# Gate and up of a SwiGLU layer by Strassen's 2 by 2 scheme, over pairs of token chunks

## The chip, the cores and the metric

One core of a Trainium2 chip runs the whole program. The metric is the device time of one execution in microseconds (us). Before the change it was 2166.83 us, the median of 3 runs that lay between 2162.72 and 2170.63.

The names of the engines are those of the profile: PE (TensorE, matmuls), PEld (its weight loads), DVE (VectorE), ACT (ScalarE), POOL (GpSimd), SP (SyncE, which here only issues DMAs). All five work through their own list of instructions in order.

## The reference

A transformer block on 2048 tokens of width 640: attention with 32 heads, then a SwiGLU layer of width 1728, each behind a layer norm and with a residual.

```python
B, S, D, H, F = 1, 2048, 640, 32, 1728
def _A_ref(x, wqkv, wo):                      # attention, Dh = 20
    q, k, v = qkv[0], qkv[1], qkv[2]
    p = _softmax(jnp.einsum("bhqd,bhkd->bhqk", q, k) * (Dh ** -0.5), axis=-1)
    o = jnp.einsum("bhqk,bhkd->bhqd", p, v)
    return o.transpose(0, 2, 1, 3).reshape(B, S, D) @ wo
def _B_ref(x, w_gate, w_up, w_down):
    g = _silu(x @ w_gate)
    u = x @ w_up
    return (g * u) @ w_down
h = x + _A_ref(_layernorm(x), A_wqkv, A_wo)
h2 = h + _B_ref(_layernorm(h), B_w_gate, B_w_up, B_w_down)
```

All is float32. The change is in `x @ w_gate` and `x @ w_up`.

## The kernel before

**Precision.** PE multiplies in the type fp32r. To keep float32's accuracy each operand is held as two fp32r parts, `hi` (a copy, rounded) and `lo` (what is left), and each product is made of three: hi by hi, lo by hi, hi by lo. `split` (L71) makes the parts: ACT writes `hi`, and POOL (or DVE, where the caller says so) subtracts and writes `lo`.

**Tiles.** The tokens are 4 chunks of 512 (`NC`, `CH`), each of 4 tiles of 128 (`TPC`). The width 640 is 5 blocks of 128 (`ND`), the inner width 1728 is 13 blocks of 128 and a last one of 64 (`NF` = 14, index f). A PSUM bank holds 128 x 512.

**Order.** The program is written in the order in which each engine is to work (`manual_schedule`), and nothing reorders it. Attention comes first and ends about 1550 us into the span. The output projection of chunks 0 and 1, their layer norm and their transposition (`projection`, L554: `project`, `apply`, `flip`) are woven into attention's last units. Chunk 2 (`two`, also called `ahead`) and chunk 3 (`three`) follow when attention is over, with the first gate products (`gate(0, c)`) between their steps to keep PE at work. The normalised, transposed tokens of a chunk, split into hi and lo, are `z2_c[c]`, five blocks of 128 x 512 for each part.

**The layer itself** (L861 to the end) runs over f, and for each f over the four chunks. `gate` (L832) makes the gate's 128 x 512 result in one bank with 15 matmuls (3 part products by 5 blocks) and the up result in another with 15 more; ACT takes Silu of the first (L849), DVE multiplies (`product`, L854), ACT and POOL split the product into `y_hi` and `y_lo` (`parts`). `down` (L917) multiplies a y of three chunks earlier by the rows of `w_down` for its f: for each of 4 token tiles two halves of 320 columns, each 3 matmuls into a bank that DVE adds to the residual `h_c[c]` (L932). For the last f, of 64, gate and up share one bank, and y has its two parts in the two halves of one tile.

**Weights.** `load_gate_up` loads 128 columns of gate and of up through one raw buffer, and ACT and POOL split them into `gu_hi` and `gu_lo`, one f ahead. They serve all four chunks, so each weight is loaded and split once. `load_down_raw` and `split_down` do the same for `w_down`. All loads go through SP's queue. There are 4 banks for gate and up (`ps_a`) and 4 for projections, transposes and down (`ps_b`).

## Time and profile before

| what | before |
|---|---|
| median of 3 runs | 2166.83 us |
| the profiled execution | 2168.25 us, of which its span is 2166.2 us |
| granted TensorE clock | 0.996 |
| share of the chain that ended last: PE | 92% |
| of it gate and up (L841) | 17% |
| of it down (L927) | 9% |
| GpSimd busy over the whole span | 15% |

The span runs from the first instruction to the last; the 2.05 us beside it lie outside the program's instructions. The profile is one execution, 1.4 us above the median of the runs.

How to read what follows. A row of a view by groups gives the source line, the engine, the operation, the tile written and the tiles read, the shapes, the count, then the busy time of the group in us and the mean of one in ns, then the idle time of that engine ahead of them and what ended it. A row of the timeline gives the start and the length in us. A matmul's end is modelled and overlaps the next one, so that what a stream of matmuls costs is read from the distance of their starts. In a window's row the busy time of each engine in that stretch stands with the number of instructions.

### The profile page before, as it was taken

To read this page: it belongs to the slowest core of one execution; us is meant where nothing else is said; L and a number is where in the kernel's file an instruction comes from. 1 tells how busy PE (TensorE), PEld (TensorE's weight loads), DVE (VectorE), ACT (ScalarE), POOL (GpSimd) and SP (SyncE) were. 2 spreads that over 40 slices of the span, in tenths; PEclk is the share of its full clock that TensorE was granted. 3 is DMA by queue.
4 is the path that set the end of the run, shared out by engine and by line. 5 is a ranking of instruction groups with operands and counts; after the bars stand their busy time and mean duration, and the time that the engine had idled before them with its cause. 6 is when DMAs were issued, how large, how long until landed. Compare 5 with 4: busy or idle time off the path is not lost.

```text
span 2166.2 us, 33813 instructions
## 1 busy us (share of the span) xinstructions
PE 2132.8 (98%) x12882; PEld 1254.5 (58%) x12882; DVE 1616.1 (75%) x2731; ACT 1277.6 (59%) x2486; POOL 317.0 (15%) x282
## 2 busy tenths in 40 slices
PE   7999999999999999999999999999999999999999
PEld 5766774333333333333333333355688888888888
DVE  6999996999999999999999999974354333544434
ACT  4222217999989999999999999977522111211110
POOL 5122212000000000000000001011223222122220
PEclk9999999999999999999999999999999999999999
DMA  7565532210302111102112122011221000010002
GB/s 250 160 178 165 164 106 80 58 48 19 87 19 61 44 36 55 48 22 79 26 47 59 49 67 53 22 58 58 77 62 37 25 25 25 19 31 25 25 19 97
DMA packets 123066, 140.06 MB, mean 65 GB/s; under 512 B 38600, under 2 KB 71624, under 8 KB 122904
## 3 DMA queue, kind: packets, MB, share of 16 engines
q1 hardware_dynamic: 109224, 111.68, 17.8%
q10 hardware_dynamic: 13680, 26.23, 4.0%
q8 instruction: 101, 1.65, 0.3%
q14 instruction: 61, 0.50, 0.1%
HBM read 99.06 MB, written 38.01 MB: 63 GB/s over the span
## 4 chain that ended last, share of the span: by engine, by line
PE 92%; DVE 5%; DMA 2%; ACT 0%; issue 0%; POOL 0%; SPq 0%; ACTq 0%; POOLq 0%; DVEq 0%
PE acc L656 23%; PE ps_a L841 17%; PE ps_max L156 15%; PE ps_one L646 13%; PE ps_b L927 9%; PE ps_one L397 5%; DVE mx L150 3%; PE ps_wide L146 2%; PE ps_one L431 2%; PE ps_max L586 2%; PE ps_b L586 1%; DVE mx L162 1%; PE ps_one L365 0%; PE ps_one L181 0%; DMA o_t<-o_d 0%
## 5 line engine op out<-in xcount | busy, mean ns | idle before, releaser
L652 ACT ACTIVATE probs<-ps_one 128x512 f32<-128x512 f32 x2048 | 1044.9, 623 | 133.6 <-PE ps_one L646 132.7
L162 DVE TENSOR_REDUCE mx<-ps_max 128x1 f32<-128x512 f32 x1632 | 1021.0, 683 | 97.9 <-PE ps_max L156 49.9
L646 PE MATMUL ps_one<-q_stk,k_stk 62*128 62x512 f32 x2048 | 551.7, 422 | 1.1 <-ACT e L240 0.7
L656 PE MATMUL acc<-probs,v_stk 128*32 128x512 f32 x4096 | 546.3, 605 | 0.2
L156 PE MATMUL ps_max<-k_stk,q_stk 60*128 60x512 f32 x1632 | 541.6, 460 | 2.5 <-DVE mx L162 1.5
L156 PEld LDWEIGHTS ps_max<-k_stk,q_stk 60*128 60x128 f32 x1632 | 230.6, 184 | 429.9 <-DVE mx L162 412.7
L932 DVE TENSOR_TENSOR h<-ps_b,h 128x320 f32<-128x320 f32 x448 | 194.6, 486 | 311.6 <-PE ps_b L927 311.5
L646 PEld LDWEIGHTS ps_one<-q_stk,k_stk 62*128 62x128 f32 x2048 | 299.7, 185 | 81.0 <-ACT probs L652 52.3
L841 PE MATMUL ps_a<-z,gu_hi 128*128 128x512 f32 x1080 | 276.0, 393 | 0.6 <-ACT z L72 0.6
L150 DVE TENSOR_REDUCE mx<-ps_wide 128x2 f32<-128x1024 f32 x208 | 240.6, 1217 | 17.8 <-PE ps_wide L146 17.4
L841 PEld LDWEIGHTS ps_a<-z,gu_hi 128*128 128x128 f32 x1080 | 200.4, 188 | 42.2 <-ACT z L72 0.8
L72 ACT ACTIVATE y_hi<-s 128x512 fp32r<-128x512 f32 (+1 forms) x56 | 35.4, 631 | 253.3 <-DVE s L854 246.8
L656 PEld LDWEIGHTS acc<-probs,v_stk 128*32 128x32 f32 x4096 | 80.9, 108 | 161.0 <-issue 152.6
L849 ACT ACTIVATE s<-ps_a 128x512 f32<-128x512 f32 (+1 forms) x56 | 33.4, 597 | 198.0 <-PE ps_a L841 198.0
L841 PE MATMUL ps_a<-z,gu_lo 128*128 128x512 f32 x540 | 142.2, 393 | 0.0
L927 PE MATMUL ps_b<-d_hi,y_hi 128*128 128x320 f32 x448 | 139.0, 311 | 0.0
L927 PE MATMUL ps_b<-d_lo,y_hi 128*128 128x320 f32 x448 | 138.1, 309 | 0.0
L927 PE MATMUL ps_b<-d_hi,y_lo 128*128 128x320 f32 x416 | 128.3, 308 | 0.0
L173 POOL CAST both<-neg 128x16 fp32r<-128x16 f32 x32 | 6.6, 206 | 806.3 <-DVE neg L169 388.1
L841 PEld LDWEIGHTS ps_a<-z,gu_lo 128*128 128x128 f32 x540 | 101.4, 188 | 23.2
L73 POOL TENSOR_TENSOR y_lo<-s,y_hi 128x512 fp32r<-128x512 f32 x52 | 67.8, 1304 | 268.9 <-ACT y_hi L72 268.9
L240 ACT ACTIVATE e<-ps_one 128x512 f32<-128x512 f32 x37 | 22.1, 596 | 119.5 <-PE ps_one L397 95.8
(118 smaller groups left out, 1623.2 us busy)
## 6 DMA issues: line engine op xcount, KB each, us to landing
raw<-qk_d SPq DMA_DIRECT2D x70, 160.0 KB
k_stk<-qk_d SPq DMA_DIRECT2D x64, 160.0 KB
q_stk<-qk_d SPq DMA_DIRECT2D x64, 160.0 KB
rb<-r_d SPq DMA_DIRECT2D x32, 256.0 KB
qk_d<-e ACTq DMA_DIRECT2D x22, 320.0 KB
v_d<-ev ACTq DMA_DIRECT2D x16, 384.0 KB
raw<-qk_d SPq DMA_DIRECT2D x70, 80.0 KB
v_stk<-v_d SPq DMA_DIRECT2D x28, 192.0 KB
```

Of the source, the lines that this page charges most:

```text
L73: lo_engine.tensor_tensor(out=lo, in0=src, in1=hi.bitcast(F32), op=ALU.subtract)
L150: nc.vector.tensor_reduce(mx[:, :, pair, t, kc], ps, axis=AX.X, op=ALU.max)
L156: nc.tensor.matmul(ps, queries[u][rows, pair, t * P : (t + 1) * P], keys[u // NC][rows, pair, kc * CH : (kc + 1) * CH], start=True, stop=True,
L162: nc.vector.tensor_reduce(mxs[u][:, b, pair, t, kc : kc + 1], ps, axis=AX.X, op=ALU.max)
L397: nc.tensor.matmul(ps, w[:, k, m * P : (m + 1) * P], a[:, k, :], start=(n == 0 and k == 0), stop=(n == 2 and k == ND - 1),)
L586: nc.tensor.matmul(ps[:, :HALF], a[:, k, :], w[:, k, hs], start=(n == 0), stop=(n == 3 * ND - 1),)
L646: nc.tensor.matmul(ps, keys[u // NC][rows, p, kt * P : (kt + 1) * P], queries[u][rows, p, :], start=True, stop=True,)
L652: nc.scalar.activation(probs[p][:, b, :], ps, AF.Exp, scale=scale)
L656: nc.tensor.matmul(acc[32 * j : 32 * j + 32, :], values[u // NC][:, kt, j * VW : j * VW + 32], probs[j // 2][:, j % 2, :], start=(kt == 0) ...
L841: nc.tensor.matmul(ps, a[:, i, k, :], b[:, k, :], start=(n == 0), stop=(n == 3 * ND - 1))
L927: nc.tensor.matmul(ps[:, :HALF], a[:, t * P : (t + 1) * P], b[:, hs], start=(n == 0), stop=(n == len(products) - 1),)
L932: nc.vector.tensor_tensor(out=h, in0=ps[:, :HALF], in1=h, op=ALU.add)
```

## The change

The gate and up products of a pair of chunks are seen as one product of 2 by 2 blocks. The weights' blocks are A11 and A12 (gate, token blocks 0 and 1, then 2 and 3) and A21 and A22 (up, the same); the tokens' blocks are B11 and B21 (the first chunk of the pair, token blocks 0 and 1, then 2 and 3) and B12 and B22 (the second chunk). In Winograd's form of the scheme seven products replace eight: of A11, A12, A22 and four sums of weights S1 to S4, with B11, B21, B22 and four sums of tokens T1 to T4. Each product is over two blocks of 128, so it takes 3 x 2 = 6 matmuls of 512 columns. The fifth block of 128 of the width is left out of the scheme and is added in the plain way by 3 matmuls for each of gate and up and each chunk ("K4").

An *element* is one f for one pair of chunks. The elements run over the pair 0 (chunks 0 and 1) with the narrow f first (done plainly, `plain`), then f = 0 to 12 (`blocks`), then the same for pair 1 (chunks 2 and 3). That gives:

- **Weights** are loaded and split twice, once for each pair (`Weights`). For each element but the narrow ones POOL makes S1 to S4 (four sums of 128 x 256, `sums`), and seven units of 128 x 256 and one of the fifth block are split by ACT and POOL, during the element ahead.
- **Results** come from seven banks: the eight sums of `blocks` are made on DVE out of PSUM (one is a copy on ACT), and the product of Silu and up (`mul`) now reads two tiles of SBUF.
- **Tokens of pair 0**: `quarter_sums` adds hi and lo back together on DVE, POOL makes the differences, ACT and DVE split them again. That stands between the projections of chunk 2.
- **Tokens of pair 1**: their layer norm, transposes, differences and splits (`late_tokens`) are moved from before the layer into elements 1 to 5, a step after every second product; the results go to DRAM (`z_d`, `t_d`). In the last element of pair 0 `swap` loads them over the tiles of pair 0, as each is read for the last time.
- **Down** of an element runs in the steps of the next, two halves of a tile behind each product (three in a narrow element). The banks are 5 for `ps_a` and 3 for `ps_b`.

The diff, cut to its core:

```diff
+    t14 = pe2.tile([P, 2, 4, CH], F32R, name="t14")
+    t32 = pe2.tile([P, 2, 4, CH], F32R, name="t32")
+        def sums(self):
...
+            tt = nc.gpsimd.tensor_tensor
+            tt(out=s1, in0=u[:, 0:2], in1=u[:, 2:4], op=ALU.add)
+            tt(out=s2, in0=s1, in1=g[:, 0:2], op=ALU.subtract)
+            tt(out=s3, in0=g[:, 0:2], in1=u[:, 0:2], op=ALU.subtract)
+            tt(out=s4, in0=g[:, 2:4], in1=s2, op=ALU.subtract)
+        def unit(self, kind):
...
+            t = self.units[kind] = pd1.tile([P, 2, 2, P], F32R, name="unit", bufs=9)
+            split(src, t[:, 0], t[:, 1], nc.gpsimd)
+        def tasks(self):
...
+            return [
+                [self.load], [], [self.sums, lambda: u("A11")], [lambda: u("S2")],
+                [lambda: u("A12"), self.last], [lambda: u("S1")],
+                [lambda: u("S3"), lambda: u("A22")], [lambda: u("S4")],
+            ]
+    def quarter_sums(j):
...
+        def back(name, z, k):
+            r[name] = tmp()
+            nc.vector.tensor_tensor(
+                out=r[name], in0=z[:, 0, k].bitcast(F32), in1=z[:, 1, k].bitcast(F32), op=ALU.add
+            )
+        def minus(out, a, b):
+            nc.gpsimd.tensor_tensor(out=r[out], in0=r[a], in1=r[b], op=ALU.subtract)
+        def keep(name, t, k):
+            split(r[name], t[:, 0, k], t[:, 1, k], nc.vector)
...
+    def blocks(w, step, done):
+        p1, ps = tmp(), bank()
+        products(ps, two_of(u["A11"]), two_of(z0))
+        nc.scalar.activation(p1, ps, AF.Copy)
+        step()
+        u2, ps = tmp(), bank()
+        products(ps, two_of(u["S2"]), two_of(t32, 2))
+        add(u2, ps, p1)
+        step()
+        ps = bank()
+        products(ps, two_of(u["A12"]), two_of(z0, 2), True, False)
+        products(ps, one_of(u["K4"], 0), one_of(z0, ND - 1), False)
+        add(p1, ps, p1)
+        nc.scalar.activation(p1, p1, AF.Silu)
+        step()
+        u5, ps = tmp(), bank()
+        products(ps, two_of(u["S1"]), two_of(t14))
+        add(u5, ps, u2)
+        step()
+        u4, ps = tmp(), bank()
+        products(ps, two_of(u["S3"]), two_of(t32))
+        add(u2, ps, u2)
+        add(u4, ps, u5)
+        step()
+        ps = bank()
+        products(ps, two_of(u["A22"]), two_of(t14, 2), True, False)
+        products(ps, one_of(u["K4"], 1), one_of(z0, ND - 1), False)
+        add(u2, ps, u2)
+        mul(u2, p1)
+        done(0, p1)
+        step()
+        ps = bank()
+        products(ps, two_of(u["S4"]), two_of(z1, 2), True, False)
+        products(ps, one_of(u["K4"], 0), one_of(z1, ND - 1), False)
+        add(u5, ps, u5)
+        nc.scalar.activation(u5, u5, AF.Silu)
+        step()
+        ps = bank()
+        products(ps, one_of(u["K4"], 1), one_of(z1, ND - 1))
+        add(u4, ps, u4)
+        mul(u4, u5)
+        done(1, u5)
+        step()
...
+    pc_ctx.close()
+    pd2 = ctx.enter_context(tc.tile_pool(name="pd2", bufs=1))
...
+        def flip(c, t):
...
+            x = zz[c] = pd2.tile([P, 4, P], F32, name="zz", bufs=4)
+            nc.scalar.activation(x, big.rearrange("p (k n) -> p k n", n=P), AF.Copy)
+            keep(small[:, :P].unsqueeze(1), z_d[c - 2][:, :, 4:5, ts_], lo_engine=nc.vector)
+            keep(x, z_d[c - 2][:, :, :4, ts_])
...
+    for e, (pair, f) in enumerate(elements):
...
+        def step():
...
+            if n == 0:
+                dn["raw"] = load_down(f)
+            for t in tasks[n]:
+                t()
+            if n == 3:
+                dn["parts"] = split_down(dn["raw"])
+            if e == NF - 1:
+                swap(n)
+            for _ in range(each):
+                if old:
+                    old.pop(0)()
+            if n % 2 and late:
+                late.pop(0)()
...
+        if e == 0:
+            for i, s in enumerate(ready):
+                done(i, s)
+            dn["parts"] = split_down(load_down(f))
+        else:
+            (plain if f == NF - 1 else blocks)(wts.pop(e), step, done)
```

**Three places in the order of instructions.** The first is POOL's list from the end of attention to the first element: `o_lo` belongs to the projections of chunks 2 and 3, `gu_lo`, `unit` and `sums` to gate and up weights, `tmp` (L889) to the token differences of pair 0. Before:

```order
L73 TENSOR_TENSOR o_lo<-o_t,o_hi 128x640 x2
L73 TENSOR_TENSOR gu_lo<-gu_raw,gu_hi 128x640
L73 TENSOR_TENSOR o_lo<-o_t,o_hi 128x640
L73 TENSOR_TENSOR gu_lo<-gu_raw,gu_hi 128x640
L73 TENSOR_TENSOR o_lo<-o_t,o_hi 128x640 x5
```

and with the change:

```order
L75 TENSOR_TENSOR o_lo<-o_t,o_hi 128x640 x2
L75 TENSOR_TENSOR unit<-raw,unit 128x256
L889 TENSOR_TENSOR tmp<-tmp 128x512 x2
L75 TENSOR_TENSOR o_lo<-o_t,o_hi 128x640
L75 TENSOR_TENSOR unit<-raw,unit 128x256
L889 TENSOR_TENSOR tmp<-tmp 128x512 x2
L75 TENSOR_TENSOR unit_19021<-raw,unit_19021 128x128
L75 TENSOR_TENSOR o_lo<-o_t,o_hi 128x640
L889 TENSOR_TENSOR tmp<-tmp 128x512 x4
L75 TENSOR_TENSOR o_lo<-o_t,o_hi 128x640 x2
```

The third and the fourth `o_lo` of chunk 2 now stand behind two differences and a unit each.

The second is PE's list in the layer. Before, one chunk's gate and up, and the start of the down that follows:

```order
L841 MATMUL ps_a<-z_3_18894,gu_hi 128x512 x5
L841 MATMUL ps_a<-z_3_18894,gu_lo 128x512 x5
L841 MATMUL ps_a<-z_3_18894,gu_hi 128x512 x10
L841 MATMUL ps_a<-z_3_18894,gu_lo 128x512 x5
L841 MATMUL ps_a<-z_3_18894,gu_hi 128x512 x5
L927 MATMUL ps_b<-d_hi,y_hi 128x320
L927 MATMUL ps_b<-d_lo,y_hi 128x320
L927 MATMUL ps_b<-d_hi,y_lo 128x320
```

With the change, a piece of an element: the product of S3 and T3, two halves of down, and the product of A22 and T4 with the fifth block (`t_18898` is `t32`, `t_18897` is `t14`, `z_0` the tokens of the pair's first chunk):

```order
L866 MATMUL ps_a<-t_18898,unit 128x512 x6
L936 MATMUL ps_b<-d_hi,y_hi 128x320
L936 MATMUL ps_b<-d_lo,y_hi 128x320
L936 MATMUL ps_b<-d_hi,y_lo 128x320
L936 MATMUL ps_b<-d_hi,y_hi 128x320
L936 MATMUL ps_b<-d_lo,y_hi 128x320
L936 MATMUL ps_b<-d_hi,y_lo 128x320
L866 MATMUL ps_a<-t_18897,unit 128x512 x6
L866 MATMUL ps_a<-z_0_3012,unit_24799 128x512 x3
```

Thirty matmuls of 512 columns in a row and 24 of 320 have become groups of 6, 9 or 3 of the one with 6 of the other between.

The third is SP's list, where the narrow f's weights are loaded. Before, in the middle of the loop:

```order
L826 DMA d_raw<-in_B_w_down 128x640
L811 DMA gu_raw<-in_B_w_gate 128x5x64
L811 DMA gu_raw<-in_B_w_up 128x5x64
L829 DMA d_raw<-in_B_w_down 64x640 x2
L806 DMA gu_raw<-in_B_w_gate 128x5x128
```

and with the change, where pair 0 ends (`z_0` and `z_1` are the tokens of the pair):

```order
L905 DMA d_raw<-in_B_w_down 128x640
L817 DMA raw<-in_B_w_gate 128x5x64
L817 DMA raw<-in_B_w_up 128x5x64
L1141 DMA z_1_3013<-z_d_64 128x2x1024
L1141 DMA z_0_3012<-z_d_63 128x2x1024
L1141 DMA t_18898<-t_d_66 128x2x1024
```

Seven more such loads follow these three, five of the same size and two of half of it, before the `w_down` rows and the weights of the next elements.

More of the change, by code (lines that the diff above doesn't have):

```diff
@@ L915, in parts, with down @@
         return y_hi, None
[L917 removed]
+    def down(c, t, half, wts, y_hi, y_lo, final):
         d_hi, d_lo = wts
         tt = c * TPC + t
[L920 removed]
+        pairs = [(y_hi, d_hi), (y_hi, d_lo)]
         if y_lo is not None:
[L922 to L934 removed]
@@ L961, in tile_block @@
-    for now in waiting:
-        for t in range(TPC):
-            down(*now, t)
+            pairs.append((y_lo, d_hi))
+        hs = slice(half * HALF, (half + 1) * HALF)
+        ps = ps_b()
+        for n, (a, b) in enumerate(pairs):
+            nc.tensor.matmul(
+                ps[:, :HALF], a[:, t * P : (t + 1) * P], b[:, hs],
+                start=(n == 0), stop=(n == len(pairs) - 1),
+            )
+        h = h_c[c][:, t, hs]
+        nc.vector.tensor_tensor(out=h, in0=ps[:, :HALF], in1=h, op=ALU.add)
@@ new lines, in tile_block @@
+    order = [NF - 1, *range(NF - 1)]
+    elements = [(pair, f) for pair in range(2) for f in order]
+    wts = {0: Weights(NF - 1), 1: Weights(0)}
+    wts[0].load()
+    two, three = ahead, projection(3, ps_b)
+    two[4]()
+    quarters = quarter_sums(0) + quarter_sums(1)
+    fill = [f for step in wts[0].tasks()[1:] for f in step]
+    for i, f in enumerate(two[1]):
+        f()
+        if i == 2:
+            reciprocals(u, r, nc.sync)
+        if i == 3:
+            rb = spread(u, nc.sync)
+        if i == 4:
+            store_o(u, o, rb, nc.vector, nc.sync)
+            three[4]()
+            three[0][0]()
+        if i >= 1 and fill:
+            fill.pop(0)()
+        quarters.pop(0)()
```

330 lines of the change are left out of this document (194 added, 136 removed).

## The prediction

> **What bounds the kernel now.** I read the views in this order: the busy time by engine, stretches of the part that changes, the starts of single matmuls, PE's waits, and then the prices of what the other engines get.
>
> ```profile
> PE 2132.8 (98%) x12882; PEld 1254.5 (58%) x12882; DVE 1616.1 (75%) x2731; ACT 1277.6 (59%) x2486; POOL 317.0 (15%) x282
> ```
>
> Two stretches (length, then busy time and count for PE, PEld, DVE, ACT, POOL, then the clock): the projections of chunk 2, and the layer; and starts of matmuls within the layer:
>
> ```profile
> 1550.94:1569.49 18.55, 18.15 (x121) 17.70 (x121) 7.11 (x18) 4.87 (x6) 7.80 (x5) 1.00 0.51 160
> 1622.09:2148.00 525.91, 525.91 (x2723) 460.58 (x2722) 212.96 (x473) 90.53 (x147) 124.34 (x88) 1.00 0.09 24
> ...
> 1709.06 1.33 PE L841 MATMUL ps_a<-z,gu_hi 128*128 128x512 f32 x5
> ...
> 1716.06 0.30 PE L927 MATMUL ps_b<-d_hi,y_hi 128*128 128x320 f32 x1
> ...
> 1719.57 1.33 PE L841 MATMUL ps_a<-z,gu_hi 128*128 128x512 f32 x5
> ```
>
> In the 526 us of the layer PE is busy all the time at full clock, DVE 40% of it, ACT 17%, POOL 24%. So here the number of matmuls sets the time. Thirty matmuls of 512 columns take 1716.06 − 1709.06 = 7.00 us, 0.2333 each; 24 of 320 take 3.51, 0.146 each, so a half of down (three) takes 0.44.
>
> **What the change removes.** A pair of chunks at one full f took 60 matmuls of 512 columns; now it takes 7 x 6 + 12 = 54. Over 13 f and 2 pairs 156 fall away: 156 x 0.2333 = **36.4 us**. Projections, transposes, down and the narrow f keep their matmuls. PE's time for an element is 54 x 0.2333 + 48 x 0.146 = 19.6 us, for a narrow one 30 x 0.2333 + 7.0 = 14.0.
>
> The waits of PE around the last transposes, which leave this place, go too (0.8 + 0.6 + 0.6 = **2.0 us**):
>
> ```profile
> PE ps_b L586 <- DVE z L73: 0.8, 1, 0.8
> PE ps_b L614 <- DVE z L602: 0.6, 2, 0.4
> PE ps_a L841 <- ACT z L72: 0.6, 1, 0.6
> ```
>
> **What it adds, and whether PE hides it.** Prices of the operations:
>
> ```profile
> L932 DVE TENSOR_TENSOR h<-ps_b,h 128x320 f32<-128x320 f32 x448 | 194.6, 486 | 311.6 <-PE ps_b L927 311.5
> L73 POOL TENSOR_TENSOR y_lo<-s,y_hi 128x512 fp32r<-128x512 f32 x52 | 67.8, 1304 | 268.9 <-ACT y_hi L72 268.9
> L73 POOL TENSOR_TENSOR d_lo<-d_raw,d_hi 128x640 fp32r<-128x640 f32 x14 | 22.2, 1583 | 63.5 <-ACT d_hi L72 63.5
> L72 ACT ACTIVATE y_hi<-s 128x512 fp32r<-128x512 f32 x52 | 32.8, 631 | 246.8 <-DVE s L854 246.8
> L602 DVE TENSOR_SCALAR z<-h,mv,r_c 128x640 f32<-128x640 f32 x16 | 9.5, 613 | 0.1
> L593 DVE BATCH_NORM_STATS2 st<-h 128x6 f32<-128x320 f32 x30 | 14.8, 495 | 1.0
> L691 DVE TENSOR_TENSOR o<-o,rb 128x512 f32<-128x512 f32 x1 | 0.7, 692 | 3.5 <-DMA rb<-r_d 3.5
> L85 DVE TENSOR_TENSOR t_c<-r_c 128x4 f32<-128x4 f32 x12 | 2.0, 163 | 0.4
> ```
>
> And for two operations of DVE, the shortest, median and longest in ns, with a piece of the timeline:
>
> ```profile
> L854 DVE TENSOR_TENSOR s<-ps_a,s x52: 679/681/691, 1579.9 to 2149.6; 128x512 f32<-128x512 f32 x52
> L858 DVE TENSOR_TENSOR s<-up,s x4: 676/1313/1530, 1881.8 to 1902.5; 64x512 f32<-64x512 f32 x4
> ...
> 1888.04 1.57 POOL L73 TENSOR_TENSOR gu_lo<-gu_raw,gu_hi 128x640 fp32r<-128x640 f32 x1 [10.50 <-ACT gu_hi L72]
> ...
> 1888.85 1.31 DVE L858 TENSOR_TENSOR s<-up,s 64x512 f32<-64x512 f32 x1
> ```
>
> POOL's work of 128 x 256 has no row: half of 1304 ns is 0.65 us, the line through the rows of 512 and 640 columns (279 ns for 128) gives 1304 − 2 x 279 = 0.75; I take 0.76. An element then costs POOL 12 x 0.76 + 1.58 + 2 x 1.30 = 13.3 us, and DVE 10 x 0.68 + 16 x 0.486 = 14.6; ACT's 14 operations come to less than 14 x 0.63 = 8.8. All lie below 19.6: over an element nothing overtakes PE. [...]
>
> The last rows tell of a collision. L858 reads two tiles of SBUF; its shortest takes 0.68 us, and one of 1.31 began 0.81 into a POOL operation of 1.57. L854, with one input in PSUM, stays between 0.68 and 0.69 in all 52. So where both operands of DVE lie in SBUF, DVE and POOL take turns: in `mul`, in the norm's `apply` and in `quarter_sums`.
>
> (1) *Steady elements.* The tightest place is the element's end. The 3 banks `ps_b` let the second half of the next element's first down start only when the add of step 8's first half is done. From the end of product 8 PE needs 0.88 (two halves) + 1.40 (product) + 0.44 = 2.72 us to get there. DVE has 0.58 of step 7 left (it trails PE by 0.2, by the rows below, and step 6 leaves it 0.3 behind), then add, `mul` and the add: 0.58 + 0.68 + 0.68 + 0.49 = 2.43. So 0.29 is spare, and a wait of `mul` for POOL of 0.4 (half a 0.76) costs 0.11 an element, x 26 = **3 us**. Bounds: 0 if POOL is idle there; a whole 0.76 each time, 0.47 x 26 = 12.
>
> ```profile
> 1559.11 0.90 PE L586 MATMUL ps_b<-wo_hi,o_lo 128*128 128x320 f32 x5
> ...
> 1560.04 0.49 DVE L592 TENSOR_TENSOR h<-ps_b,h 128x320 f32<-128x320 f32 x1 [0.69 <-PE ps_b L586]
> ```
>
> (Five such matmuls pass on after 0.73, at 1559.84, and DVE starts at 1560.04.)
>
> (2) *Projections of chunk 2.* POOL's third `o_lo` now stands behind two differences, and these behind sums on DVE, whose start waits for the residual:
>
> ```profile
> 1556.13 0.49 DVE L592 TENSOR_TENSOR h<-ps_b,h 128x320 f32<-128x320 f32 x1 [5.62 <-DMA h<-in_A_x]
> 1560.43 1.57 POOL L73 TENSOR_TENSOR o_lo<-o_t,o_hi 128x640 fp32r<-128x640 f32 x1 [2.94 <-ACT o_hi L72]
> 1564.42 1.59 POOL L73 TENSOR_TENSOR o_lo<-o_t,o_hi 128x640 fp32r<-128x640 f32 x1
> 1566.56 0.89 PE L586 MATMUL ps_b<-wo_hi,o_lo 128*128 128x320 f32 x5
> ```
>
> From 1556.1: add and statistics 1.0, two sums (as L691) 1.4, add and statistics 1.2, two sums in turn with the first difference 2.7, the second difference 1.3 gives 1563.7; then the third `o_lo`, 1565.3 against 1562.0 before. Then a unit, two differences, a small unit and three splits in turn, 0.76 + 2.6 + 0.5 + 2.1 = 6.0, and the fourth `o_lo`: 1572.9, which the projection that used it at 1566.56 awaits: **6 us**. Bounds 2 (the turns do not clash) and 10 (the second group holds up chunk 3's first tile as well).
>
> (3) *Into element 1.* The first `w_down` rows now go to memory that the projections' weights leave, so their load starts after the last projection. The nearest load of 320 KB was issued at 1557.52 and used at 1562.08:
>
> ```profile
> 1557.52 0.38 SPq L806 DMA_DIRECT2D gu_raw<-in_B_w_up  x1
> ...
> 1562.08 0.74 ACT L72 ACTIVATE gu_hi<-gu_raw 128x640 fp32r<-128x640 f32 x1 [1.74 <-DMA gu_raw<-in_B_w_up]
> ```
>
> So 4.6, then the copy 0.74 and POOL's 1.58, against one product of 1.4 as cover: 5.5. That load shared the queue with others; I take **5**, bounds 4 and 6. In element 1 the moved norms add 28 small operations of 0.16 and two `apply` to DVE, 14.6 + 4.6 + 1.5 = 20.7 against PE's 12.6 + 4.7 = 17.3; banks absorb some 2.4: **1** (0 to 3).
>
> (4) *Elements 2 to 5.* They carry the late tokens. Ten transposes take PE 1.0 us:
>
> ```profile
> 1576.49 1.25 PE L614 MATMUL ps_b<-ident,z 128*128 128x128 f32 x10
> 1577.50 1.41 PE L841 MATMUL ps_a<-z,gu_hi 128*128 128x512 f32 x5
> ```
>
> So PE has 20.6; on POOL 4 x 1.30 + 4 x 0.76 = 8.2 more, 21.5; if every `mul` and `apply` also holds POOL up, 24.1. Over four elements POOL falls behind by 3.6 to 14. What waits for it first is the first chunk's `y_lo`: product 6 ends 14.2 into an element, add, `mul`, copy and subtraction with 0.2 make 17.7, and PE asks for it at 19.6 + 1.4 + 0.3 = 21.3. So 3.6 is spare, and the cost is 0 to 10. I take **6**: where POOL is the fuller engine it will seldom step aside for nothing.
>
> (5) *Change of pair.* 9 MiB come from DRAM while `down` and the last products run. The nearest loads are the program's first; in the view of its first 60 us, slices of 1.5 us:
>
> ```profile
> DMA  0798999997990079975399996669897988754855
> GB/s 0 189 364 237 343 369 361 348 331 190 370 358 34 0 158 365 341 184 175 33 303 337 367 280 235 224 202 298 265 269 292 246 280 272 219 173 134 228 167 187
> ```
>
> At 360 GB/s 9.44 MB take 26 us from about 2.5 us into element 13, so the last piece is there at some 30, when the narrow element needs it (19.6 + 10.2). The next weights, 1 MB more, land at 33, then 3.0 of sums and 0.76 of a unit: 36.9 against 34.4 when PE gets there (19.6 + 14.0, and 0.8 of waiting). **3**; bounds 0 and, at the 250 GB/s of the page's first slice, 15.
>
> The sum: −36.4 − 2.0 + 3 + 6 + 5 + 1 + 6 + 3 = −14.4 us. The profiled execution took 2168.25 (span 2166.2 and 2.05 around it), so 2153.9; it was 1.4 above the median, 2166.83, so the forecast for the median is **2152 us**.
>
> **Rivals.** *(A) All is hidden.* Only the sure waits remain, 2 of (2) and 4 of (3): −38.4 + 6 gives 2134. For it: every engine has 5 us to spare in a plain element. Against: DVE stands behind POOL in (2) whatever is spare.
>
> [...]
>
> *(C) The loads at the change of pair are slow.* At 250 GB/s (5) costs 15 for 3: 2164, no change that can be told. For it: the row above goes down to 130. Against: the high slices, 340 to 370, show what the queue carries when it is full, and these loads fill it.
>
> **How the numbers follow.** A change under 0.3% (6.5 us) cannot be told from none: faster is below 2160.3, slower above 2173.3. Forecast 0.58 (its own range 2142 to 2164: faster 0.44, same 0.11, slower 0.03), A 0.17 (faster), B 0.13 (slower), C 0.12 (same 0.08, slower 0.04). Together faster 0.61, same 0.19, slower 0.20. The range for 8 in 10 reaches down to A and up into C, 2134 to 2174.
>
> **What would show it.** Right: 1464 matmuls of 512 columns for gate and up; stretches of 19.6 us in elements 6 to 12 and in pair 1, with PE busy throughout; PE idle in four places, the projections of chunk 2 (behind `o_lo`), the first down (behind `d_lo`), elements 2 to 5 (behind `y_lo` or units) and the narrow element of pair 1 (behind a load). Wrong: `mul` at a mean above 1.6 us with PE waiting on `ps_b` in every element is B; elements of 20.5 us or more in pair 1 undo the forecast; PE waiting over 8 us on loads of z or t tiles is C; no idle at the four places is A.

## The result, and the profile after

Over 12 runs each the changed kernel takes a median of 2168.5 us (2165.26 to 2171.9), the kernel before 2166.03: a ratio of 1.0014, with a 95% interval of 1.0002 to 1.0026. Forecast were 2152 us. By the 0.3% that the prediction set, the change cannot be told from the kernel before. All ratios here compare fast runs alone, which leaves out one of the 12 runs of n1_norms below (5418.87 us). The profiled execution took 2166.65 us, its span 2164.9.

The page's first part, busy time by engine, and five stretches of the changed kernel (columns as before: length, then PE, PEld, DVE, ACT, POOL, then the clock, the DMA share and GB/s). The stretches are the projections of chunk 2, element 1, elements 3 to 5, elements 8 to 13, and elements 14 and 15:

```profile
PE 2107.7 (97%) x12726; PEld 1231.7 (57%) x12726; DVE 1770.9 (82%) x2947; ACT 1364.2 (63%) x2737; POOL 578.9 (27%) x627
```

```profile
1545.14:1567.94 22.80, 18.70 (x120) 17.72 (x121) 14.63 (x28) 5.44 (x10) 14.47 (x11) 1.00 0.42 121
1595.31:1630.24 34.93, 24.25 (x93) 19.55 (x92) 26.09 (x60) 7.60 (x16) 12.42 (x14) 0.80 0.17 48
1651.89:1718.43 66.54, 63.15 (x332) 54.21 (x333) 45.38 (x87) 27.06 (x62) 62.59 (x69) 1.00 0.51 147
1761.83:1878.95 117.12, 117.12 (x614) 102.99 (x613) 79.93 (x157) 35.26 (x80) 73.60 (x84) 1.00 0.30 94
1878.95:1918.26 39.31, 34.89 (x167) 29.74 (x165) 24.19 (x47) 12.77 (x28) 19.82 (x24) 0.91 0.64 216
```

PE has 156 matmuls fewer (12726 for 12882) and 25 us less of busy time, but its busy share fell from 98% to 97%: it waits. The fourth row is a steady stretch, where PE is busy for all of 117.12 us at full clock. The others are not: in element 1 PE works 24.25 of 34.93 us, at a mean clock of 0.80, and in elements 3 to 5 POOL is busy 62.59 of 66.54.

The starts of the first product of elements 16, 17 and 18 in the timeline of PE:

```profile
1918.26 1.56 PE L866 MATMUL ps_a<-z,unit 128*128 128x512 f32 x6
...
1938.28 1.56 PE L866 MATMUL ps_a<-z,unit 128*128 128x512 f32 x6
...
1957.80 1.56 PE L866 MATMUL ps_a<-z,unit 128*128 128x512 f32 x6
```

A steady element takes 1957.80 − 1938.28 = 19.52 us. Before, four chunks of one f took 41.72 us (starts at 1709.06 and 1750.78), so a pair took 20.86. The matmuls that were taken out are nearly a gain in full there: 1.34 us of the 1.40 counted for each element. What PE waits for from 1545 us on (total, times, longest):

```profile
PE ps_b L936 <- DVE h L941: 7.1, 5, 3.7
PE ps_b L1097 <- DVE h L941: 4.2, 4, 1.2
PE ps_b L936 <- POOL y_lo L75: 3.6, 4, 2.5
PE ps_b L588 <- POOL o_lo L75: 3.4, 2, 1.8
PE ps_b L936 <- ACT d_hi L74: 3.1, 1, 3.1
PE ps_b L588 <- ACT o_hi L74: 2.8, 3, 1.8
PE ps_a L866 <- DMA z<-z_d: 2.7, 1, 2.7
PE ps_b L936 <- POOL d_lo L75: 1.9, 2, 1.0
PE ps_b L588 <- ACT o L668: 0.7, 1, 0.7
```

29.5 us of waits; before, the layer had 3.1 of them. And behind a long wait the matmuls come at half the pace. PE at the head of element 6:

```profile
1718.43 1.56 PE L866 MATMUL ps_a<-z,unit 128*128 128x512 f32 x6
...
1722.81 0.64 PE L936 MATMUL ps_b<-d_hi,y_lo 128*128 128x320 f32 x1 [2.52 <-POOL y_lo L75]
...
1724.04 2.57 PE L866 MATMUL ps_a<-t,unit 128*128 128x512 f32 x6
1726.45 0.31 PE L936 MATMUL ps_b<-d_hi,y_hi 128*128 128x320 f32 x1
```

Six matmuls that pass on after 1.40 us at 1718.43 take 1726.45 − 1724.04 = 2.41. The granted clock says why. These are the four stretches of the layer in which it was at a half while PE still had matmuls to do (the sixth figure behind the length):

```profile
1599.96:1606.78 6.82, 5.78 (x16) 4.79 (x17) 2.30 (x5) 0.56 (x1) 1.54 (x1) 0.50 0.53 145
1620.44:1627.26 6.82, 6.05 (x17) 5.08 (x18) 6.04 (x11) 1.48 (x4) 2.21 (x2) 0.50 0.00 1
1722.84:1726.25 3.41, 3.41 (x10) 2.95 (x11) 0.99 (x2) 0.00 (x0) 3.41 (x5) 0.50 0.53 152
1886.68:1893.50 6.82, 6.22 (x18) 5.48 (x19) 2.50 (x5) 1.82 (x3) 0.00 (x0) 0.50 1.10 299
```

Before, there was none in the layer ahead of PE's last matmul. The lengths are 3.41 us once and 6.82 three times, and the one of 3.41 followed a wait of 2.52 us.

**Where the gain went.** For each place the first column is PE's own work (matmuls by their distances: 120 x 0.146 for the projections of a chunk, 19.52 for a plain element, 0.5 for five transposes; elements 1 and 15 do the shorter downs of a narrow element, 32 matmuls for 48, and have 17.3 without transposes), the second the distance between the first matmul of this place and of the next:

| place | PE's work | taken | lost | forecast |
|---|---|---|---|---|
| projections of chunk 2 | 17.6 | 22.8 | 5.2 | 6, term (2) |
| narrow element, projections of chunk 3 | 24.6 | 27.4 | 2.8 | none |
| element 1 | 17.8 | 34.9 | 17.1 | 6, term (3) |
| elements 2 to 6 | 101.2 | 112.1 | 10.9 | 6, term (4) |
| elements 7 to 13 and 17 to 26 | | | 0 | 3, term (1) |
| elements 14 to 16, the change of pair | 50.8 | 59.3 | 8.5 | 3, term (5) |
| sum | | | 44.5 | 24 |

From the end of attention to the end of the span the kernel before takes 2166.2 − 1550.94 = 615.3 us, the changed one 619.7 (from 1545.14 to 2164.9). That is 4.5 more, where −36.4 − 2.0 + 44.5 makes 6.1; the kernel before had small losses of its own beside those 2.0 (its waits of PE alone are 3.1). Attention itself, the same code, ended anywhere from 1544.7 to 1555.1 in the profiled executions of this study; so profiles are compared below by this later part, called the layer, and times by their ratio over 4 to 12 runs (f2_all 4; e3_late, a1_quiet and f1_all 6).

### The profile page after: what moved, and what is told of

Same layout as the page of the kernel before. It is cut to its first block, busy times and chain, and to the rows that moved or that the text cites. A ratio compares the mean times of both kernels' runs of the same rounds, so it can differ in the third digit from the quotient of the medians.

```text
span 2164.9 us, 34835 instructions
## 1 busy us (share of the span) xinstructions
PE 2107.7 (97%) x12726; PEld 1231.7 (57%) x12726; DVE 1770.9 (82%) x2947; ACT 1364.2 (63%) x2737; POOL 578.9 (27%) x627
## 4 chain that ended last, share of the span: by engine, by line
PE 87%; DVE 6%; DMA 3%; POOL 2%; issue 1%; ACT 1%; SPq 0%; ACTq 0%; POOLq 0%; DVEq 0%
PE acc L658 23%; PE ps_max L158 15%; PE ps_a L866 14%; PE ps_one L648 14%; PE ps_b L936 8%; PE ps_one L399 5%; DVE mx L152 3%; PE ps_one L433 2%; PE ps_wide L148 2%; PE ps_max L588 2%; DMA z<-z_d 1%; DVE mx L164 1%; POOL unit L75 0%; DMA qk_d<-e 0%; PE ps_one L367 0%
## 5 line engine op out<-in xcount | busy, mean ns | idle before, releaser
L648 PEld LDWEIGHTS ps_one<-q_stk,k_stk 62*128 62x128 f32 x2048 | 299.6, 185 | 80.4 <-ACT probs L654 52.3
L985 DVE TENSOR_TENSOR tmp<-ps_a,tmp 128x512 f32<-128x512 f32 x208 | 141.3, 690 | 138.6 <-PE ps_a L866 134.4
L866 PE MATMUL ps_a<-z,unit 128*128 128x512 f32 x840 | 221.9, 400 | 2.7 <-DMA z<-z_d 2.7
L866 PEld LDWEIGHTS ps_a<-z,unit 128*128 128x128 f32 x840 | 156.5, 192 | 31.0 <-DMA z<-z_d 3.0
L866 PE MATMUL ps_a<-t,unit 128*128 128x512 f32 x624 | 163.1, 397 | 0.0
L74 ACT ACTIVATE y_hi<-tmp 128x512 fp32r<-128x512 f32 (+1 forms) x56 | 35.3, 631 | 167.1 <-DVE tmp L986 153.4
L866 PEld LDWEIGHTS ps_a<-t,unit 128*128 128x128 f32 x624 | 114.5, 191 | 18.7
L999 ACT ACTIVATE tmp<-tmp 128x512 f32<-128x512 f32 x26 | 16.4, 633 | 130.0 <-DVE tmp L985 130.0
L936 PEld LDWEIGHTS ps_b<-d_hi,y_hi 128*128 128x128 f32 x448 | 85.8, 191 | 21.5 <-DVE h L941 8.5
```

Source lines behind the costliest of these rows:

```text
L648: nc.tensor.matmul(ps, keys[u // NC][rows, p, kt * P : (kt + 1) * P], queries[u][rows, p, :], start=True, stop=True,)
L866: nc.tensor.matmul(ps, w[k][:, i], z[k][:, j], start=(first and m == 0), stop=(last and m == len(n) - 1),)
L936: nc.tensor.matmul(ps[:, :HALF], a[:, t * P : (t + 1) * P], b[:, hs], start=(n == 0), stop=(n == len(pairs) - 1),)
L985: add = lambda out, ps, x: nc.vector.tensor_tensor(out=out, in0=ps, in1=x, op=ALU.add)
```

## The experiments

Three theories stand in the expectations. Theory 1: the gain on PE is whole and is given back by waits at the places above, each long one followed by a stretch at half clock; what takes a wait away gains both. Theory 2: only the waits count. Theory 3: the added work costs its time wherever it stands.

Element numbers and stages are those above. All lengths in the table are distances of first matmuls in the profile of each kernel; the time is the ratio to the kernel before, run on the same chip, with its 95% interval. The element 7 to 13 column would be 136.6 with no late tokens in it and nothing in the way.

| kernel | proj. 2 to 3 | el. 1 | el. 2–6 | el. 7–13 | el. 14–16 | layer | ratio |
|---|---|---|---|---|---|---|---|
| the change | 50.2 | 34.9 | 112.1 | 136.6 | 59.3 | 619.7 | 1.0014 (1.0002–1.0026) |
| e1_shift | 51.8 | 29.1 | 114.3 | 136.6 | 59.0 | 617.4 | 1.0012 (1.0000–1.0024) |
| e2_norms | 52.0 | 27.4 | 119.4 | 136.6 | 60.5 | 622.4 | 1.0030 (1.0018–1.0042) |
| e3_late | 50.2 | 28.9 | 116.5 | 146.1 | 60.4 | 628.8 | 1.0046 (1.0029–1.0064) |
| e4_swap | 52.3 | 33.5 | 112.9 | 136.6 | 59.1 | 621.1 | 1.0015 (1.0003–1.0027) |
| w1_warm | 52.4 | 32.0 | 111.8 | 136.6 | 59.1 | 618.5 | 1.0015 (1.0006–1.0025) |
| a1_quiet | 52.5 | 24.5 | 103.1 | 139.4 | 59.7 | 605.8 | 0.9946 (0.9931–0.9960) |
| o1_outs | 50.4 | 34.9 | 114.3 | 136.6 | 55.5 | 618.5 | 1.0013 (1.0002–1.0024) |
| f1_all | 51.9 | 24.6 | 103.1 | 139.4 | 58.1 | 603.8 | 0.9948 (0.9934–0.9963) |
| n1_norms | 52.0 | 26.7 | 110.2 | 136.6 | 60.0 | 612.2 | 0.9984 (0.9971–0.9996) |
| s1_split | 51.5 | 33.3 | 101.8 | 139.4 | 59.8 | 612.3 | 0.9982 (0.9973–0.9991) |
| f2_all | 51.1 | 20.3 | 103.3 | 139.5 | 53.7 | 594.6 | 0.9896 (0.9884–0.9909) |

Elements 17 to 27 take 226.5 or 226.6 in all of them. The projections (the first column) take from 50.2 to 52.5 us in kernels in which their code is the same, so differences of 2 us in that column mean nothing.

### One edit at a time

**e1_shift**: the down products of element 1 begin two steps later.

```diff
+        skip = 2 if e == 1 else 0
+        each = -(-len(pending) // (steps - skip))
-            for _ in range(each):
+            for _ in range(each if n >= skip else 0):
```

> Element 1 alone: the downs of the narrow element start behind its third product in place of its first (3 halves a step for 2). In the changed kernel PE idles 4.1 us before the first down (3.1 for d_hi, 1.0 for d_lo), and the clock is halved for 6.83 us from 1599.96 on. Theory 1 (waits, and half clock behind each long one): some 2.7 of the 4.1 go, for d_lo lands about 1.4 us after the third product ends, and the halved window goes too, 3.4 us of work: 6 us faster than the changed kernel, some 2162. Theory 2 (waits alone; the slow matmuls behind them have another cause): 2.7 us. Theory 3 (the added work costs its time wherever it stands): nothing.

**e2_norms**: the scales of the norms of chunks 2 and 3 (14 small operations of DVE each) ahead of element 1.

```diff
             dn["parts"] = split_down(load_down(f))
+            late.pop(0)()
+            late.pop(0)()
```

> The 28 small norm operations of chunks 2 and 3 go from element 1 to the place behind the last projection, where VectorE is idle for 4 us. In the changed kernel PE idles 1.6 and 3.7 us in element 1 for VectorE's additions, and the clock is halved for 6.83 us from 1620.44 on. Theory 1: both waits shrink to under 1 us and that window goes, 4.5 + 3.4 = 8 us faster than the changed kernel, some 2160. Theory 2: 4.5 us. Theory 3: nothing, since VectorE has the same operations.

**e3_late**: two late items an element in place of four.

```diff
-            if n % 2 and late:
+            if n % 4 == 3 and late:
```

> The late tokens' steps come after every fourth product in place of every second, in elements 1 to 10 for 1 to 5. GpSimd then gets 4.1 us more an element in place of 8.2, some 17.5 of 19.5 us. Theory 1: the waits for y_lo (3.6 us) and most of those of the transposes (4.2) go, and the halved window of 3.41 us at 1722.84: 6 to 9 us faster than the changed kernel, some 2161. Theory 2: 5 to 7. Theory 3: nothing, the work is only spread.

**e4_swap**: another order of the loads at the change of pair; the sums of tokens come last, in element 14.

```diff
-                swap(n)
+                swap(("B12 B11", "", "B21", "", "", "K0", "B22", "K1")[n])
+            if e == NF and n == 1:
+                swap("T2 T1 T3 T4")
```

> At the change of pair the pieces that the narrow element reads are loaded first (B11, B12, B21, K0, B22, K1), then the next weights, and the four token sums last. In the changed kernel PE idles 2.7 us for the fifth block, 0.9 for d_lo and 1.1 for additions, and the clock is halved for 6.83 us from 1886.68 on. Theory 1: the wait for the load and the window go, 2.7 + 3.4 = 6 us faster than the changed kernel, some 2162; if the token sums come late for element 15, a wait there takes some of it back. Theory 2: 2.7. Theory 3 (the loads' own time): nothing, the bytes are the same.

None brought what was expected. e3_late was slower than the change; e2_norms may have been, but the two intervals overlap. Each time one place became shorter (element 1 by 5.8, 7.6 and 6.0, elements 14 and 15 by 5.5), and later places took all or a part of it back. In e2_norms and e3_late it is one and the same thing. Waits in the head of element 6 of e3_late:

```profile
DVE tmp L985 <- ACT tmp L989: 5.5, 1, 5.5
ACT kept L74 <- POOL zz L1114: 4.9, 1, 4.9
...
PE ps_b L936 <- DVE h L941: 2.4, 1, 2.4
```

These are read from the second row up: both edits move the item `sums` to an element's last step. There ACT reaches its copy `kept` and stands 4.9 us behind the four differences that POOL has still to make. Queued behind `kept` is ACT's first eviction of the next element (L989); DVE's first add waits 5.5 us for that, the adds of down stand behind it on DVE, and PE finds no free bank of `ps_b`. The same three figures (5.5, 4.9, 2.4) stand in element 3 of e2_norms. So the reading is that the place of one item in ACT's queue, not the amount of work, cost these two some 3 to 5 us at each `sums`; n1_norms and s1_split below test it.

In e4_swap elements 14 and 15 gain 5.5 us and element 16 loses 5.3. SP's queue in e4_swap (start, length), and the windows of elements 15 and 16:

```profile
1893.16 12.07 SPq L943 DMA_DIRECT2D out<-h  x7
1907.26 0.34 SPq L905 DMA_DIRECT2D d_raw<-in_B_w_down  x1
```

```profile
1900.66:1918.95 18.29, 17.57 (x88) 14.77 (x87) 13.48 (x26) 5.86 (x14) 7.91 (x12) 1.00 0.69 260
1918.95:1944.23 25.28, 21.70 (x105) 18.26 (x103) 14.89 (x27) 8.32 (x20) 19.64 (x23) 0.93 0.19 53
```

Seven output stores, each waiting for the sum it stores, hold the queue for 12.07 us ahead of the weights of element 16. POOL has only 7.91 us of work in element 15 and 19.64 in element 16, when the weights are there.

### Is the halved clock a cost of its own?

**w1_warm**: the waits stay, but PE is kept at work in them with products that nothing reads.

```diff
+    BEFORE = {(1, 0): 18, (1, 3): 6, (1, 5): 15, (6, 0): 10}
+    BEHIND = {(1, 7): 5, (NF, 1): 11}
+        def spin(count):
+            ps = bank()
+            w, z = cur.units["A11"][:, 0, 0], z2_c[0][:, 0, 0]
+            for _ in range(count):
+                nc.tensor.matmul(ps, w, z, start=True, stop=True)
```

> The changed kernel with idle-filling matmuls: at six places where PE waited in its profile (twice 18 and 15 and once 6 matmuls in element 1, 10 in element 6, 5 and 11 at the ends of element 1 and in element 14) as many 128x512 products of operands long ready are issued that nothing reads; output unchanged. Every wait stays. Theory 1 (a wait of PE costs its own length and then a stretch at half clock): the four half-clock stretches of the layer (23.9 us at clock 0.5 in the profile of the change) go, elements 1, 6 and 14 come to about 28, 22 and 17 us from 34.9, 23.9 and 19.8, and the time falls by 8 to 12 us to about 2158. Theory 2 (waits alone; the doubled matmuls have another cause): the same places keep their time, 2168 to 2172. Theory 3 (the added work costs its time wherever it stands): 2168 plus the dummies, 2175 or more.

The four half-clock stretches went. Element 1 and the head of element 6, as windows:

```profile
1600.00:1628.00 28.00, 26.35 (x123) 21.46 (x122) 21.45 (x53) 5.92 (x12) 9.56 (x11) 1.00 0.21 59
1722.00:1727.00 5.00, 4.21 (x21) 3.35 (x20) 1.79 (x4) 2.98 (x8) 5.00 (x6) 1.00 0.72 203
```

The time did not: 1.0015. Element 1, with 13.64 us at half clock fewer (6.8 us of PE's pace), is only 2.9 shorter. In the middle of it DVE decides: from its first small operation to the end of the second chain it takes 12.7 us here and 12.6 in the change. Element 6, where PE alone decides, gains 1.0 (22.9 for 23.9). The added products did not themselves hold PE up: behind those at the head of element 1 PE still waited 0.45 us, and behind those of element 6 0.79. Two stretches of 3.41 us at half clock came up in the projections instead, so the whole time says little here and the places say more. So the half of theory 1 that priced each stretch at its full loss fell: in element 1 2.9 us came back for 6.8 of PE's pace, and in element 6, where PE is the bound right behind the wait, 1.0 of at most 23.88 − 19.52 − 2.52 = 1.8 us.

### Several places at once

**a1_quiet**: norms ahead of element 1 with their two places left empty, so that no other item moves; later downs; `sums` in two items, so that ACT meets `kept` when POOL is done; half the density behind element 1.

```diff
+            late.pop(0)()
+            late.pop(0)()
+            late[:0] = [lambda: None, lambda: None]
+        skip = 2 if e == 1 else 0
-            keep(a, t_d[0][:, :, :, ts_])
-            keep(b, t_d[1][:, :, :, ts_])
+        def keeps(t):
+            ts_ = slice(t * P, (t + 1) * P)
+            keep(zz[2], t_d[0][:, :, :, ts_])
+            keep(zz[3], t_d[1][:, :, :, ts_])
+            items.append(lambda t=t: keeps(t))
-            if n % 2 and late:
+            if (n % 2 if e == 1 else n % 4 == 3) and late:
```

> The changed kernel with four edits to element 1 and the late tokens: both norms' scales are made ahead of element 1 with their two places in the queue left empty (so that the other items keep theirs), element 1's down products start two steps later, the differences of the late tokens and their splits are two items in place of one, and behind element 1 two items are issued an element in place of four. In the singles the time of an element moved but came back elsewhere: POOL was busy 21.95 of 23.0 us in elements 2 to 5 of the change, and where the items were thinned ACT stood behind POOL's differences (4.93 us) and held the next eviction. Theory 1 (waits at named places, each with its half clock): element 1 goes from 34.9 to about 21, elements 2 to 11 together from 209.7 to about 204, the time to about 2150. Theory 2 (waits only, no clock): half of that, 2160. Theory 3 (the engines' work costs its time wherever it is put): 2166 to 2170.

2153.45 us, 0.9946: here the time fell, nearly to the 2150 of theory 1. That number held the full price of the halved clock, which w1_warm does not bear out, so that it came so near is in part luck. Elements 2 to 11 together took 203.6 us, from 209.7.

**o1_outs**: the new order of loads, and each output store put into the queue one step later.

```diff
-            nc.sync.dma_start(out[tt * P : (tt + 1) * P, :], h_c[c][:, t, :])
+            outs.append((out[tt * P : (tt + 1) * P, :], h_c[c][:, t, :]))
+            put_out()
             if n == 3:
```

> The changed kernel with the new order of the pair's loads (B12, B11, B21, K0, B22, K1 in element 13, the four sums in element 14), and with each output store put into SP's queue one step after the product it stores rather than right behind it. With the order alone elements 14 and 15 fell from 39.3 to 33.9 us and element 16 rose from 20.0 to 25.3: eight stores held SP's queue for 12.07 us, the weights of element 16 were asked for at 1908.1 and its first unit was split 5.24 us late. Theory 1: with the stores no longer in the way element 16 comes back to about 20 and elements 14 to 16 together to 54 from 59.3: 5 us less than the change, 2163. Rival: the transfers themselves (eight stores of 327 KB beside the loads) are what is late, and element 16 stays at 24 to 25: 2167 to 2169.

Elements 14 to 16 came to 55.5 us, near the 54 of theory 1, with element 16 at 21.8, between the two expectations. But element 6 took 25.6 in this profile, from 23.9, and the ratio, 1.0013, cannot be told from that of the change.

**f1_all**: a1_quiet, o1_outs, and `quarter_sums` with each operation one step behind its inputs.

```diff
-            lambda: (back("22", z1, 2 + j), back("21", z0, 2 + j), minus("11", "12", "11"),
-                     minus("12", "22", "12")),
-            lambda: (minus("22", "22", "11"), minus("21", "21", "22"), keep("11", t14, j)),
-            lambda: (keep("12", t32, j), keep("22", t32, 2 + j), keep("21", t14, 2 + j)),
+            lambda: (back("22", z1, 2 + j), back("21", z0, 2 + j), minus("11", "12", "11")),
+            lambda: (keep("11", t14, j), minus("12", "22", "12"), minus("22", "22", "11")),
+            lambda: (keep("12", t32, j), minus("21", "21", "22")),
+            lambda: (keep("22", t32, 2 + j), keep("21", t14, 2 + j)),
```

> All of the edits of a1_quiet and o1_outs, and the quarter sums of the tokens put one step apart from their inputs (each difference on POOL takes what VectorE made a step earlier, each split what POOL made a step earlier), so that ACT and POOL don't stand behind them while the projections of chunk 2 wait. Theory 1: projections of chunks 2 and 3 go from 42.8 to about 38, element 1 to about 21, elements 14 to 16 to about 54, the layer from 619.7 to about 594 us, and the time to about 2142. Theory 2 (no clock): about 2155. Theory 3: 2166 to 2170.

No better than a1_quiet. The new order of the quarter sums did not help the projections (51.9 us for 52.5), and element 16 took 24.7 again. Six of the stores still held SP's queue for 8.64 us, from 1875.81 on, and moved beside the loads of the pair; the weights of element 16, asked for from 1889.30 on, kept POOL waiting until 1897.60.

### What a1_quiet is made of, and a further step

**n1_norms** has the first edit of a1_quiet alone (the three lines with `late`), **s1_split** the last two.

> One part of a1_quiet alone: both norms' scales ahead of element 1, with their two places in the queue of late items left empty, so that each later item keeps its step (in e2_norms they moved up two places and elements 2 to 5 rose by 11.7 us). Theory 1 in the form that it has after w1_warm (the lost time of element 1 is VectorE's: the first w_down, then two chains of 14 small operations ahead of the additions that free PE's banks; the halved clock falls into waits and costs little of its own): element 1 about 27 us from 34.9, elements 2 to 6 as in the change (112.1 together), the time about 2161. Theory 3 (the work costs its time wherever it stands, so only the thinning of the late items helped a1_quiet): 2167 to 2169.

> The other part of a1_quiet alone: two late items an element in place of four from element 2 on, and differences and splits of the late tokens as two items; norms where the change has them. Theory 1: element 1 stays at about 35, elements 2 to 11 together go from 209.7 to about 203.5 us, the time to about 2162. Theory 3 (the same work, only spread): 2167 to 2169. If n1_norms and s1_split each give their part, the two and the later start of the down products account for the 15 us of a1_quiet.

Both came out as theory 1 had it, and they bear the reading of ACT's queue out: with the norms moved but each later item left in its step, elements 2 to 5 take 88.2 us as in the change, against 99.9 in e2_norms; with the items thinned but `sums` in two, elements 2 to 11 take 202.2, against 223.6 in e3_late. n1_norms: element 1 at 26.7 us, 8.2 less, nothing lost behind it, the time at 2163.87 (0.9984). s1_split: 2162.76 (0.9982), and 7.5 us less in elements 2 to 11. Against the 1.0014 of the change the two ratios fall by 0.0030 and 0.0032, and a1_quiet, with the later downs too, by 0.0068.

**f2_all**: f1_all with three more edits. They were not run one by one; each is read at its own place.

```diff
-            split(o, o_hi, o_lo, nc.gpsimd)
+            split(o, o_hi, o_lo, nc.vector if c == 3 or (c == 2 and t == 3) else nc.gpsimd)
+        if n3 == 2:
+            early.append(rstd_of(pe2, mvs[2][:, :, 1], TPC, "c2"))
-            put_out()
+            if e > NF + 1:
+                put_out()
```

> f1_all with three more edits: the low parts of the tokens of chunk 3, and of the last of chunk 2, made on VectorE (it idles half of that stage) rather than on GpSimd behind the weights of element 1; the scale of chunk 2 made during the projections of chunk 3; the output stores of the first pair held until element 16 and issued one a step, since in f1_all they moved beside the pair's loads at 380 to 427 GB/s and the weights of element 16 took 7 us to land. Theory 1 (each wait at its place): projections of chunks 2 and 3 with the plain element from 51.9 to about 47 us, element 1 from 24.6 to about 21, element 16 from 24.7 to about 20; the layer from 603.8 to about 590, the time to about 2141. [...]

2145.13 us, 0.9896 (0.9884 to 0.9909): faster than the kernel before and than the change. The windows of the projections of chunk 2, of element 1, and of the change of pair, and then SP's queue:

```profile
1548.55:1569.90 21.35, 18.87 (x121) 17.72 (x121) 14.38 (x25) 5.44 (x10) 11.27 (x9) 1.00 0.45 129
1599.66:1619.98 20.32, 18.70 (x93) 15.06 (x92) 18.64 (x44) 7.39 (x15) 10.15 (x11) 1.00 0.29 80
...
1863.00:1917.00 54.00, 52.26 (x269) 44.77 (x268) 37.92 (x73) 19.18 (x42) 35.68 (x42) 1.00 0.61 208
```

```profile
1865.14 3.44 SPq L1154 DMA_DIRECT2D t<-t_d  x4
...
1883.47 0.37 SPq L812 DMA_DIRECT2D raw<-in_B_w_gate  x1
...
1900.62 6.30 SPq L949 DMA_DIRECT2D out<-h  x8
```

The clock stands at 1.00 in all three: no stretch of the layer ahead of PE's last matmul is at a half any more. Element 1 is at 20.3 (17.8 of PE's work), element 16 at 19.8, with its weights asked for at 1883.47 and the stores only from 1900.62 on. The edit of `o_lo` missed: the projections of chunks 2 and 3 with the narrow element still take 51.1 us against 42.2 of PE's work, PE now waiting 3.8 us for `o_lo` of DVE. That stage stays open.

## Why the prediction was wrong

**The gain: right.** A pair of chunks has 54 matmuls for 60, and the steady elements take 19.52 us (19.6 forecast). Neither rival A (waits only at the sure places) nor B (`mul` waits for POOL in every element) came. Term (1) forecast 3 us from a mean wait of `mul` for POOL of 0.4 us, and there is no wait of PE in the stretch of 117.12 us. In it `mul` took the same time in all 12 cases and did not wait (shortest, median and longest in ns):

```profile
L986 DVE TENSOR_TENSOR tmp<-tmp x12: 691/692/693, 1761.9 to 1874.5; 128x512 f32<-128x512 f32 x12
```

The operation that grew there was POOL's: six of the 12 began 0.07 us ahead of a `unit` of 128 x 256, and those six took 1.21 or 1.22 us, other such units 0.74.

**The step that failed is the pricing of the waits, 24 us of them where 44.5 came, and 11 of the 20 that were missing lie in term (3).** The time of 2168.5 us lies within the stated range, 2134 to 2174, but the upper part of that range was there for slow loads (C), which did not come; that it holds is luck. No term had a halved clock in it either, 23.9 us of which came with the waits. The first half of term (3) was right: 5 us for the first `w_down`, where PE waited 3.1 for `d_hi` and 1.0 for `d_lo`. Its second half set the moved norms in element 1 against PE as a load ("14.6 + 4.6 + 1.5 = 20.7 against PE's 12.6 + 4.7 = 17.3; banks absorb some 2.4: **1** (0 to 3)"). What happened is a matter of order. DVE in element 1 of the change:

```profile
1602.30 1.02 DVE L941 TENSOR_TENSOR h<-ps_b,h 128x320 f32<-128x320 f32 x2 [4.15 <-PE ps_b L936]
...
1606.87 0.16 DVE L80 TENSOR_SCALAR v_c<-mv 128x4 f32<-128x4 f32 x1
1607.06 0.68 DVE L82 TENSOR_SCALAR r_c<-v_c 128x4 int32<-128x4 int32 x1
...
1614.70 1.49 DVE L82 TENSOR_SCALAR r_c<-v_c 128x4 int32<-128x4 int32 x1
...
1619.48 1.28 DVE L985 TENSOR_TENSOR tmp<-ps_a,tmp 128x512 f32<-128x512 f32 x2
```

DVE idles for 4.15 us, since the first down waits for the first `w_down`; then the first chain of small operations holds its queue from 1606.87 to 1611.47 and the second from 1614.26 to 1619.48, 4.6 and 5.2 us, and the adds that free PE's banks stand behind each. One load that comes late and two blocks behind it add up; a sum of busy times sees none of that. n1_norms measured the norms' part at 8.2 us in the element. With the scale of chunk 2 made during the projections, and the downs later, 20.3 us are left.

**Term (4), 6 us, was mis-sized: 10.9.** Its mechanism is right: POOL was busy 62.59 of 66.54 us in elements 3 to 5, and `y_lo` is awaited where it was said, at the head of an element (2.52 us in element 6). What it left out is the adds of down behind the late tokens (PE's transposes waited 4.2 us for them, 1.2 of it in element 1). Thinning the items and parting `sums` gave 7.5 us back.

**Term (5), 3 us, was mis-sized: 8.5.** The load that is awaited is the one foreseen, with 2.7 us for z where 0.8 was forecast; with it came 6.82 us at half clock, and the two together are most of the loss. The rate was not the reason: it was mostly above the 360 GB/s taken. In the view of the transfers from 1863 to 1890 us, in slices of 0.7 us:

```profile
GB/s 231 104 371 399 382 376 388 413 419 376 358 206 249 334 334 370 425 425 401 431 431 401 419 431 407 407 413 407 407 385 404 404 404 407 404 394 388 347 222 211
```

So rival C (slow loads) fell. Not foreseen either was SP's queue behind the loads, the output stores ahead of the next weights, which cost element 16 5.3 us once the loads were put in another order (e4_swap). f2_all measured the three elements at 53.7.

**Term (2), 6 us, came out near its size: 5.2.** Its chain was right in part. The third `o_lo`, behind the differences, was awaited for 1.58 us. But for the fourth tile PE waited longest for `o_hi`, in ACT's queue, which the term does not have: it stands there behind two copies `t` that wait for POOL's differences.

```profile
1560.58 0.63 ACT L74 ACTIVATE t<-tmp 128x512 fp32r<-128x512 f32 x1 [3.70 <-POOL tmp L889]
1561.94 0.63 ACT L74 ACTIVATE t<-tmp 128x512 fp32r<-128x512 f32 x1 [0.73 <-POOL tmp L889]
1562.48 0.72 ACT L74 ACTIVATE o_hi<-o_t 128x640 fp32r<-128x640 f32 x1
...
1563.25 1.00 PE L588 MATMUL ps_b<-wo_hi,o_hi 128*128 128x320 f32 x5 [1.84 <-ACT o_hi L74]
```

The projections of chunk 3, which it left out, lost 2.8 more with the narrow element.

So the work that was taken from PE was given back as waits, at places where an engine's queue held something urgent behind something slow. The experiments gave 25 of the 44.5 us back (the layer from 619.7 to 594.6) without taking work away from any engine. For element 1, the late tokens and the change of pair that is shown; what would mend the projections stays open. Not tried was the same care on the kernel before; its layer had 3.1 us of PE's waits to be won.

## What to carry to other kernels

Price work that is moved to idle engines by where it stands in their queues, not by their busy share: ask at each step what urgent instruction stands behind it, and what it waits for itself. When one wait is mended, look at the next element for it before you call it won: four single edits shortened their place by 5 to 8 us each, and none the kernel. Where a queue item waits for another engine (a copy behind sums, a store behind its result), make it an item of its own a step later.

## What the runs showed of the hardware

**Half clock after short waits.** In the change a wait of 2.52 us came with 3.41 us at half clock, and waits of 3.08, 3.72 and 2.72 us came with 6.82 us each; the stretches began as the wait ended or up to 0.77 us before. In f1_all a wait of 1.85 us in the projections of chunk 3 had slow matmuls behind it too: from 1594.24 to 1596.90 two groups of five came 1.34 and 1.32 us apart, where 0.73 is usual; while the 1.84 us in the projections of chunk 2 of the change brought none. So the length of the wait alone did not decide. The four stretches shown above start 20.48, 102.40 and 163.84 us from one another, which is 6, 30 and 48 times 3.413 us, the length of the shortest. Counted in pieces of 3.413 us from 1599.96 on, both ways, PE of the change idled for 3.08, 2.95, 2.52 and 2.12 us in the pieces just ahead of the four, and for at most 1.60 us in any other from 1545 us to its last matmuls. The wait of 1.84 us, from 1561.41 to 1563.25, lay in two pieces, parted at 1562.41, with 1.00 and 0.84 us idle. This is a count of one profile; what sets the clock it does not show.

**Small operations stretched.** Operations of DVE on 128 x 4 mostly took 0.16 us. L82, with one input in SBUF, took 0.68 and 1.49 us in the change, and 0.17 in w1_warm, where its first one came while POOL was idle. The two long ones began at 1607.06 and 1614.70, and the operations of POOL that had just begun ran until 1607.71 and 1616.16:

```profile
1606.97 0.74 POOL L827 TENSOR_TENSOR sums<-raw 128x256 f32<-128x256 f32 x1 [5.40 <-DMA raw<-in_B_w_up]
...
1614.60 1.56 POOL L75 TENSOR_TENSOR d_lo<-d_raw,d_hi 128x640 fp32r<-128x640 f32 x1
```

Each ended within 0.03 us of the operation of POOL. So these two operations of a kind that took 0.17 us where POOL was idle lasted until the one of POOL beside them was done; what held them no run here shows.
